# Five rows of wo, each loaded as one stretch of 32 KB or as 16 parts of 1984 bytes and 16 of 64

## The chip, the core and the metric

The kernel runs on one core of a Trainium2 chip. The metric is the device time of one execution, in microseconds (us). Times are medians of several executions; one more execution was recorded by the profiler, and its trace is what the views show. "Span" is the time from the first to the last instruction of that recorded execution, and every start in a view counts from the span's start.

## What is computed

One token (x, 512 wide) goes through two branches, which a gate mixes: attention over a cache of 4096 positions with 32 heads of 128, and a two-layer network with a squared ReLU. All data are bf16.

```
g = sigmoid((x * gate_w).sum(-1))
q = (x @ wq).reshape(32 heads, 128)
scores[h] = k_cache[h] @ q[h] * 128 ** -0.5        # 4096 positions
o[h] = softmax(scores[h]) @ v_cache[h]
a = o.reshape(4096) @ wo                           # wo: 4096 x 512
b = relu(x @ w1 + b1) ** 2 @ w2 + b2               # 512 -> 1376 -> 512
out = g * a + (1 - g) * b
```

Nearly all of the bytes are K and V (32 heads of 1 MB each, twice); wq and wo are 4 MB each, w1 and w2 1.4 MB each.

## The kernel before

The kernel is written engine by engine: each engine has a list of its own, and semaphores tie the lists together.

**Loads.** SyncE (SP) issues wq, then the K and V loads of all heads, K seven heads ahead of V (`load_k` L262, `load_v` L267). Each is one DMA of 1024 KB onto 128 partitions, 8 KB a partition. K and V each have 8 buffers; a K load waits until head h-8 is done with (`s_sd`, `s_t`), a V load until the products of head h-8 are (`s_pv`). Between these loads SP issues w1 (after head 8), the first part of w2 (after head 10), ten pieces of wo (with heads 20 to 24), and behind the last V load the rest of w2 (L294, L295) and the last quarter of wo into the freed K buffer 0 (L297, two DMAs). The output goes out at L301.

**wo.** The first 24 heads' part of wo is 96 rows of 32 KB in the view `woa_v` (one row is 32 rows of wo side by side). Each row goes onto one partition of `W`, the buffer that wq has left. Which row goes to which partition is a table: 13 runs are issued by GpSimd (`RUNS`, L326), 5 groups of three rows by SP (`FIRST`, L279: three partitions of 4 x 8 KB), and 5 single rows by SP (`REST`, L283), onto the partitions 12, 13, 14, 15 and 44. With each of the heads 20 to 24 SP issues V of that head, K seven heads on, one `FIRST` group and one `REST` row, in this order. The ten SP pieces count on one semaphore, `s_wr`.

**A head's work.** VectorE makes half of the scores from K in place (`ttr`, L634), TensorE transposes the other half of K (L435), ScalarE copies it out (L369), and TensorE multiplies it by q (L446). After the maximum and the exponentials (L640, L643, L380) TensorE makes the product with V (`pv`, L471), seven heads behind K. In TensorE's list, step i holds `transposes(i)`, `scores(i-1)` and `pv(i-7)`, so it waits at K of head i and then at V of head i-7.

**The end.** At step 33 the outputs of the first 24 heads are spread over the partitions (L503). From there the attention's first 24 heads go through wo: TensorE takes 23 of the 32 blocks (`out_a`, L515, in steps 34 to 38), VectorE the other 9 (`part_y`, L681 and L684), whose sum TensorE adds in step 37 (`sum_y`, L543). Both wait for all pieces of `W` first (`s_wp`, `s_wr`). `sum_y` stands behind `pv(30)` and ahead of `out_a(5)` and `pv(31)`. Then come the norm of the last 8 heads (L661), their turn (L521, L717, L525, L719), the rest of w2 (L552), the last quarter of wo (`out_b`, L534), the bias (L722), a transpose (L597, L724) and the output.

Of the kernel before, what the change touches and what calls it, by code (L numbers as in the profile page):

```python
# [5 lines left out]
def bass_gated_mix__gqa_block_cached__dense_activation_squared_relu__decode_kernel(  # L6
# [58 lines left out]
    FIRST = [(INNER, 0, 3, 0, 1), (INNER, 0, 3, 1, 1), (INNER, 0, 3, 2, 1), (INNER, 0, 3, 3, 1),  # L65
             (OUTER, 0, 3, 0, 1)]
    REST = [12, 13, 14, 15, 44]
# [11 lines left out]
    def turns():  # L79
        at, out = 0, []  # L80
        for _, e, k, _, _ in RUNS:
            d = (e - at) % 16
            out.append((False, d) if d != 1 else (True, e))
            at = (e + k) % 16
        return out
# [14 lines left out]
    woa_v = A_wo.rearrange("(p t) n -> p (t n)", t=32)  # L100
# [5 lines left out]
    with ctx:  # L106
        def sb(name, shape, dt):
            return ctx.enter_context(nc.sbuf_tensor(name, shape, dt))
# [4 lines left out]
        def sem(name):  # L113
            return ctx.enter_context(nc.semaphore(name))
# [3 lines left out]
        W = sb("W", [128, 4 * 4096], bf16)  # L118
# [72 lines left out]
        s_wr = sem("s_wr")  # L191
# [61 lines left out]
        @block.sync  # L253
        def _(eng):
            for t in range(4):
                eng.dma_start(wq_sb[:, t, :], wq_v[:, t, :]).then_inc(s_wq[t], 16)  # L256

            def load_k(h):
                if h >= NK:
                    eng.wait_ge(s_sd, h - NK + 1)  # L260
                    eng.wait_ge(s_t, 2 * (h - NK + 1))
                eng.dma_start(Kt[:, h % NK, :], k_h[h, :, :]).then_inc(s_k[h % NK], 16)  # L262

            def load_v(h):
                if h >= NV:
                    eng.wait_ge(s_pv, h - NV + 1)
                eng.dma_start(Vt[:, h % NV, :], v_h[h, :, :]).then_inc(s_v[h % NV], 16)  # L267

            for h in range(LAG):
                load_k(h)  # L270
            for h in range(NH):
                load_v(h)
                if h + LAG < NH:
                    load_k(h + LAG)
                if h == HF:
                    eng.wait_ge(s_qps, 8)
                if HF <= h < HF + len(FIRST):
                    p, st, k, q = STRIPS[len(RUNS) + h - HF]
                    eng.dma_start(W[p:p + st * (k - 1) + 1:st, :], woa_v[q:q + k, :],  # L279
                                  max_dma_last_dim=8192).then_inc(s_wr, 16)  # L280
                if HF <= h < HF + len(REST):
                    p, _, _, q = STRIPS[len(RUNS) + len(FIRST) + h - HF]
                    eng.dma_start(W[p:p + 1, :], woa_v[q:q + 1, :],  # L283
                                  max_dma_last_dim=2048).then_inc(s_wr, 16)
                if h == 8:
                    eng.wait_ge(s_z, 1)
                    eng.wait_ge(s_b2, 1)
                    for t in range(4):
                        eng.dma_start(w1_sb[:, t, :], w1_v[:, t, :]).then_inc(s_w1, 16)
                if h == 10:  # L290
                    eng.dma_start(w2a[:, 0:GS[1], :], w2_v[:, 0:GS[1], :]).then_inc(s_w2[0], 16)
            eng.wait_ge(s_sd, NA + 1)
            eng.wait_ge(s_t, 2 * (NA + 1))
            eng.dma_start(w2b[:, :], B_w2[FG * 128:F, :]).then_inc(s_w2[1], 16)  # L294
            eng.dma_start(w2a[:, GS[1]:FG, :], w2_v[:, GS[1]:FG, :]).then_inc(s_w2[2], 16)  # L295
            for c in range(len(TS) - 1):
                eng.dma_start(wob_sb[:, TS[c]:TS[c + 1], :],  # L297
                              wob_v[:, TS[c] * DM:TS[c + 1] * DM].rearrange("p (t n) -> p t n", n=DM))\
                   .then_inc(s_wo[c], 16)
            eng.wait_ge(s_f4, 1)  # L300
            eng.dma_start(out[0, 0, :].rearrange("(j p) -> j p", p=128), fin4[:, :]).then_inc(s_out, 16)  # L301
            eng.wait_ge(s_out, 16)
# [92 lines left out]
        def _(eng):  # L395
# [111 lines left out]
            def out_a(n):  # L507
                if n == 0:
                    eng.wait_ge(s_ac, 2)
                    for q in s_wp:  # L510
                        eng.wait_ge(q, 16)
                    eng.wait_ge(s_wr, 16 * (len(FIRST) + len(REST)))
                for t in range(4 * n, min(4 * n + 4, TD)):
                    for j in range(4):
                        eng.matmul(acc[:, j:j + 1], wo_sb[:, t, j * 128:(j + 1) * 128],  # L515
                                   o2A[:, t:t + 1], start=False, stop=False,
                                   skip_group_check=True)
# [42 lines left out]
            for i in range(NH + LAG):  # L560
# [12 lines left out]
                if i == 34:  # L573
                    out_a(0)
                if 34 <= i < 39:
                    out_a(i - 33)
# [24 lines left out]
        def _(eng):  # L601
# [16 lines left out]
            def qcol_copy(c):  # L618
                eng.wait_ge(s_q, c + 1)
                eng.tensor_copy(qcol[:, 4 * c:4 * c + 4], Q).then_inc(s_qc, 1)  # L620
# [6 lines left out]
            def ttr(h):  # L627
                eng.wait_ge(s_k[h % NK], 16 * (h // NK + 1))
                eng.wait_ge(s_qb, h // 4 + 1)
                if h >= NS:  # L630
                    eng.wait_ge(s_e, h - NS + 1)
                for b in range(XB):
                    kb = Kt[:, h % NK, b * 128:(b + 1) * 128]
                    ins = eng.tensor_tensor_reduce(kb, kb, qb[:, h * 128:(h + 1) * 128], 1.0, 0.0,  # L634
                                                   ALU.mult, ALU.add, S[:, h % NS, b:b + 1])
                ins.then_inc(s_sd, 1)

            def smax(h):
                eng.wait_ge(s_s2, h + 1)
                eng.tensor_copy(S[:, h % NS, XB:NB], S2).then_inc(s_cp, 1)  # L640
                eng.wait_ge(s_cp, h + 1)
                eng.wait_ge(s_sd, h + 1)
                eng.tensor_reduce(mp[:, h:h + 1], S[:, h % NS, :], AX.X, ALU.max).then_inc(s_mp, 1)  # L643

            def gmax(g):
                eng.wait_ge(s_mt, g + 1)
                eng.tensor_reduce(gm[:, g:g + 1], MT[0:G, :], AX.X, ALU.max).then_inc(s_gm, 1)
                eng.wait_ge(s_gm, g + 1)
                eng.tensor_scalar(dg[:, g, :], identf[0:G, 0:G], gm[:, g:g + 1], -SCALE, ALU.mult, ALU.mult)\
                   .then_inc(s_dg, 1)  # L650

            def recip(c):
                a, b = HPO * c, HPO * c + HPO
                eng.wait_ge(s_den, c + 1)
                eng.reciprocal(rden[:, a:b], DEN[:, a:b]).then_inc(s_rd, 1)

            def norm(c):
                a, b = HPO * c, HPO * c + HPO
                eng.wait_ge(s_rd, c + 1)
                eng.wait_ge(s_pv, b)  # L660
                eng.scalar_tensor_tensor(out=onorm[:, a:b], in0=O(a, b), scalar=gcol[:, 0:1],  # L661
                                         in1=rden[:, a:b], op0=ALU.mult, op1=ALU.mult)\
                   .then_inc(s_on, 1)
# [23 lines left out]
            for i in range(NH + LAG):  # L687
                if i < NH:
                    ttr(i)
                if 1 <= i <= NH:  # L690
                    smax(i - 1)
                if i % 3 == 2 and i // 3 + 1 < 8:
                    qcol_copy(i // 3 + 1)
                if i >= 5 and (i - 5) % 4 == 0 and (i - 5) // 4 < NG:
                    gmax((i - 5) // 4)
                if i >= 12 and (i - 12) % HPO == 0:
                    recip((i - 12) // HPO)
                if i >= LAG + 1 and (i - LAG - 1) % HPO == HPO - 1:
                    norm((i - LAG - 1) // HPO)
                if i == 25:  # L700
                    mlp()
                if i == 32:
                    eng.wait_ge(s_at, 1)
                    eng.tensor_copy(oA[:, :], KP[2][0:NA, 0:128]).then_inc(s_ac, 1)
                if i == 33:
                    eng.wait_ge(s_at, 2)
                    eng.tensor_copy(o2A[:, :], O2A).then_inc(s_ac, 1)
                    eng.wait_ge(s_e, NS * 2)
                    eng.tensor_copy(o2D, O2A[:, TD:32]).then_inc(s_y2, 1)
                    for q in s_wp:  # L710
                        eng.wait_ge(q, 16)
                    eng.wait_ge(s_wr, 16 * (len(FIRST) + len(REST)))
                    eng.wait_ge(s_y2, 1)
                    part_y()
            norm(NH // HPO - 1)
# [37 lines left out]
```

## Time and profile before

| what | value |
|---|---|
| median of 3 runs | 207.82 us (207.66 to 207.99) |
| the profiled execution | 207.87 us |
| its span | 206.1 us |
| bytes moved by DMA | 78.76 MB, mean 382 GB/s |
| DMA engines in slices 2 to 36 of 40 | busy 90% or more |
| busy share of PE, DVE, ACT, POOL | 65%, 67%, 39%, 15% |
| TensorE clock granted, mean | 0.58 |

The views used are these. The page gives the span in 40 slices with the mean busy share of the core's 16 DMA engines, the DMA queues with their packets, and the chain of work that ended last. The table of windows gives for each stretch the busy time of each engine, the granted TensorE clock, the share of the 16 DMA engines that was busy, and GB/s. The timeline gives instructions in order of time: start, duration, engine, line, operation, operands, and in brackets how long the engine had been idle and what ended that. "SPq" is SyncE's queue of DMA issues; its durations are the issue alone, not the transfer.

### The profile page before, as it was taken

The numbers are of one execution on the slowest core, as the hardware profiler recorded it, in microseconds if no ns is written. First come the engines' busy times: TensorE is split into PE (matmuls) and PEld (weight loads), VectorE is DVE, ScalarE is ACT, GpSimd is POOL, SyncE is SP. The second block draws the span as 40 slices with busy tenths as digits, with TensorE's granted clock in tenths as the row PEclk, the third lists the DMA queues.
The fourth block names the chain that finished last, engine by engine and source line by source line (L and its number), as shares of the span: only waits on it lengthen the run. The fifth ranks groups of instructions, "written<-read, shape, count | busy, mean of one in ns | idle before, by whom it ended". The sixth has DMA issues, their size and how long they took to land.

```text
span 206.1 us, 6574 instructions
## 1 busy us (share of the span) xinstructions
PE 133.4 (65%) x2405; PEld 118.5 (57%) x2405; DVE 138.7 (67%) x1151; ACT 79.6 (39%) x148; POOL 30.6 (15%) x56
## 2 busy tenths in 40 slices
PE   0139577699967667266596727689987606457585
PEld 0107456287865665156466727579986606447584
DVE  0308999999997687078557737776799926445901
ACT  2106836395553445133363316330763306112000
POOL 2000000000000000000069700001987500000000
PEclk9999957555555855555555555555555555555555
DMA  6999999999999999999999999999999999999100
GB/s 238 425 428 425 418 420 421 415 426 412 421 418 415 423 400 431 409 424 423 413 426 410 420 406 411 417 404 417 407 417 406 407 420 409 420 411 366 64 35 11
DMA packets 12652, 78.76 MB, mean 382 GB/s; under 512 B 2423, under 2 KB 2521, under 8 KB 3546
## 3 DMA queue, kind: packets, MB, share of 16 engines
q1 hardware_dynamic: 11149, 75.83, 89.6%
q0 software_dynamic: 1456, 2.50, 3.3%
q8 instruction: 19, 0.31, 0.6%
q14 instruction: 14, 0.11, 0.1%
q10 hardware_dynamic: 14, 0.01, 0.0%
HBM read 78.32 MB, written 0.00 MB: 380 GB/s over the span
## 4 chain that ended last, share of the span: by engine, by line
DMA 75%; DVE 13%; PE 6%; SPq 4%; issue 1%; ACT 0%; DVEq 0%
DMA Kt<-in_A_k_cache_dram 55%; DMA Vt<-in_A_v_cache_dram 14%; DVE Kt L634 11%; DMA W<-in_A_wq_dram 5%; SPq L267 2%; SPq L262 1%; PE KP L435 1%; PE pQ L413 1%; PE pQ L471 1%; PE pX L543 1%; DVE S L634 1%; SPq L256 1%; PE pX L534 0%; PE pO L471 0%; ACT qb L361 0%
## 5 line engine op out<-in xcount | busy, mean ns | idle before, releaser
L634 DVE CUSTOM_DVE_ANT_0 Kt<-Kt,qb 128x128 bf16<-128x128 bf16 x512 | 113.3, 291 | 33.7 <-DMA Kt<-in_A_k_cache_dram 33.7
L369 ACT ACTIVATE kT<-KP 128x1024 bf16<-128x1024 bf16 x64 | 61.9, 1021 | 77.9 <-PE KP L435 77.9
L435 PE MATMUL KP<-ident,Kt 128*128 128x128 bf16 x512 | 56.1, 297 | 42.9 <-DMA Kt<-in_A_k_cache_dram 42.9
L435 PEld LDWEIGHTS KP<-ident,Kt 128*128 128x128 bf16 x512 | 48.8, 138 | 45.6 <-DMA Kt<-in_A_k_cache_dram 44.5
L634 DVE DVE_READ_ACCUMULATOR2_ANT S<- 128x1 f32 x512 | 42.0, 82 | 0.0
L446 PE MATMUL pS<-qcol,kT 128*128 128x1 bf16 x512 | 19.2, 167 | 8.4 <-DVE S L640 8.4
L446 PEld LDWEIGHTS pS<-qcol,kT 128*128 128x128 bf16 x512 | 18.9, 107 | 9.8 <-DVE S L640 9.8
L323 POOL DMA_DIRECT2D xb<-in_B_w_dram x9 | 5.4, 598 | 102.8 <-PE pQ L413 102.8
L413 PE MATMUL pQ<-W,xb 128*128 128x512 bf16 x32 | 14.9, 621 | 6.3 <-DMA W<-in_A_wq_dram 6.3
L471 PEld LDWEIGHTS pO<-E,Vt 128*128 128x128 bf16 x512 | 15.5, 104 | 1.1 <-issue 0.8
L471 PE MATMUL pO<-E,Vt 128*128 128x1 bf16 x512 | 16.1, 165 | 0.0
L341 POOL TENSOR_SCALAR_AFFINE_SELECT w_sb<-w_sb 24x36 bf16<-24x36 bf16 (+6 forms) x23 | 12.1, 528 | 3.7 <-POOL w_sb L341 0.5
L471 PE MATMUL pQ<-E,Vt 128*128 128x1 bf16 x256 | 8.0, 165 | 5.7 <-DMA Vt<-in_A_v_cache_dram 5.7
L471 PEld LDWEIGHTS pQ<-E,Vt 128*128 128x128 bf16 x256 | 7.6, 104 | 6.3 <-issue 6.0
L361 ACT ACTIVATE qb<-pQ 128x512 bf16<-128x512 f32 x8 | 4.7, 591 | 15.1 <-PE pQ L413 15.1
L380 ACT ACTIVATE E<-S,nM 128x32 bf16<-128x32 f32 x32 | 9.9, 310 | 0.3
L413 PEld LDWEIGHTS pQ<-W,xb 128*128 128x128 bf16 x32 | 3.6, 130 | 10.8 <-issue 10.8
L471 PEld LDWEIGHTS pX<-E,Vt 128*128 128x128 bf16 x256 | 7.9, 105 | 0.7 <-issue 0.6
L471 PE MATMUL pX<-E,Vt 128*128 128x1 bf16 x256 | 8.1, 166 | 0.0
L326 POOL DMA_DIRECT2D W<-in_A_wo_dram x13 | 7.3, 564 | 0.0
L640 DVE COPY S<-pS 128x16 f32<-128x16 f32 x32 | 5.4, 170 | 2.4 <-PE pS L446 2.4
L620 DVE CAST qcol<-pQ 128x4 bf16<-128x4 f32 x8 | 1.2, 153 | 8.4 <-PE pQ L421 8.4
(83 smaller groups left out, 90.1 us busy)
## 6 DMA issues: line engine op xcount, KB each, us to landing
Kt<-in_A_k_cache_dram SPq DMA_DIRECT2D x32, 1024.0 KB, 27.6
Vt<-in_A_v_cache_dram SPq DMA_DIRECT2D x32, 1024.0 KB, 28.8
W<-in_A_wq_dram SPq DMA_DIRECT2D x4, 1024.0 KB, 7.7
W<-in_A_wo_dram POOLq DMA_DIRECT2D x2, 768.0 KB, 12.9
w_sb<-in_B_w_dram SPq DMA_DIRECT2D x4, 344.0 KB, 22.7
w2a<-in_B_w_dram SPq DMA_DIRECT2D x1, 896.0 KB, 21.2
Kt<-in_A_wo_dram SPq DMA_DIRECT2D x1, 768.0 KB, 24.2
W<-in_A_wo_dram POOLq DMA_DIRECT2D x9, 64.0 KB, 23.0
```

Of the source, the lines that this page charges most:

```text
L323: eng.dma_start(dm[0:d, sent, :, 0:8], src[:, :, 0:8]).then_inc(s_dm[sent], 16)
L326: eng.dma_start(W[p:p + st * (k - 1) + 1:st, :], woa_v[q:q + k, :], max_dma_last_dim=8192).then_inc(s_wp[n], 16)
L341: eng.affine_select(out=part, in_=part, compare_op=ALU.not_equal, fill=1.0, base=-st * q, pattern=[[st, 4], [-1, st * (k - 1) + 1]], chann ...
L361: eng.activation(qb[:, c * 512:(c + 1) * 512], pQ[:, :], ACT.Copy).then_inc(s_qb, 1)
L369: eng.activation(kT[:, h % 2, j * HB * 128:(j + 1) * HB * 128], KP[n % 3][:, :], ACT.Copy).then_inc(s_ev, 1)
L380: eng.activation(E[:, h % NE, :], S[:, h % NS, :], ACT.Exp, bias=nM[:, h:h + 1], scale=SCALE, accum_out=RS[:, h:h + 1]).then_inc(s_e, 1)
L413: mm = eng.matmul(pQ[:, :], xb[:, t, :], wq_sb[:, t, c * 512:(c + 1) * 512], start=(t == 0), stop=(t == 3))
L435: mm = eng.transpose(KP[n % 3][:, y * 128:(y + 1) * 128], Kt[:, h % NK, b * 128:(b + 1) * 128], ident[:, :])
L446: mm = eng.matmul(S2[:, y:y + 1], kT[:, h % 2, y * 128:(y + 1) * 128], qcol[:, h:h + 1], start=True, stop=True)
L471: mm = eng.matmul(O(h, h + 1), Vt[:, h % NV, b * 128:(b + 1) * 128], E[:, h % NE, b:b + 1], start=(b == 0), stop=(b == NB - 1))
L634: ins = eng.tensor_tensor_reduce(kb, kb, qb[:, h * 128:(h + 1) * 128], 1.0, 0.0, ALU.mult, ALU.add, S[:, h % NS, b:b + 1])
L640: eng.tensor_copy(S[:, h % NS, XB:NB], S2).then_inc(s_cp, 1)
```

## The change

Each of the five single rows (`REST`) is seen as 16 pieces of 1024 elements, on both sides. One DMA takes the first 992 elements of every piece (1984 bytes), a second the last 32 (64 bytes). So each row is 32 stretches instead of one, and SP issues two DMAs instead of one. The same bytes go to the same partitions, and the place in SP's list is the same. The two waits for `s_wr` (in `out_a` on TensorE, and ahead of `part_y` on VectorE) count the five more DMAs.

```
-                    eng.dma_start(W[p:p + 1, :], woa_v[q:q + 1, :],
-                                  max_dma_last_dim=2048).then_inc(s_wr, 16)
+                    to, of = [m.rearrange("p (s n) -> p s n", s=16) for m in (W[p:p + 1, :], woa_v[q:q + 1, :])]
+                    for x, y in ((0, 992), (992, 1024)):
+                        eng.dma_start(to[:, :, x:y], of[:, :, x:y]).then_inc(s_wr, 16)
...
-                    eng.wait_ge(s_wr, 16 * (len(FIRST) + len(REST)))
+                    eng.wait_ge(s_wr, 16 * (len(FIRST) + 2 * len(REST)))
```

SP's list around the first of the five rows, before and now (`Kt` and `Vt` are the buffers of K and V, `W` that of wo; the line numbers behind the change are one higher):

```order
 L262 DMA Kt<-in_A_k_cache_dram 128x4096
 L279 DMA W<-in_A_wo_dram 3x4x4096
-L283 DMA W<-in_A_wo_dram 1x16384
+L285 DMA W<-in_A_wo_dram 1x16x992
+L285 DMA W<-in_A_wo_dram 1x16x32
 L267 DMA Vt<-in_A_v_cache_dram 128x4096
 L262 DMA Kt<-in_A_k_cache_dram 128x4096
 L279 DMA W<-in_A_wo_dram 3x4x4096
-L283 DMA W<-in_A_wo_dram 1x16384
+L285 DMA W<-in_A_wo_dram 1x16x992
+L285 DMA W<-in_A_wo_dram 1x16x32
```

One issue has become two, at the same place; no other instruction of any engine has moved.

More of the change, by code (lines that the diff above doesn't have):

```diff
@@ L711, in _ @@
                         eng.wait_ge(q, 16)
-                    eng.wait_ge(s_wr, 16 * (len(FIRST) + len(REST)))
+                    eng.wait_ge(s_wr, 16 * (len(FIRST) + 2 * len(REST)))
                     eng.wait_ge(s_y2, 1)
```

## The prediction

> **What bounds the kernel now.** I read the page first (the slices, the queues, the chain), then windows over the end, then the timelines of TensorE, VectorE and SyncE's issues. The page's slices, queues and chain:
>
> ```profile
> span 206.1 us, 6574 instructions
> ...
> DMA  6999999999999999999999999999999999999100
> ...
> q1 hardware_dynamic: 11149, 75.83, 89.6%
> q0 software_dynamic: 1456, 2.50, 3.3%
> ...
> DMA 75%; DVE 13%; PE 6%; SPq 4%; issue 1%; ACT 0%; DVEq 0%
> ```
>
> The DMA engines are busy from the second slice to the end of the 36th, and three quarters of the chain that ended last are loads. TensorE and VectorE follow the loads. What matters is thus when the last loads land, and the end shows that they do not land on all 16 engines alike. Windows over the end (after the counts of the five engines come the TensorE clock, the busy share of the 16 DMA engines, and GB/s):
>
> ```profile
> 178.00:190.00 12.00, 8.23 (x200) 7.61 (x201) 6.43 (x44) 3.44 (x11) 0.00 (x0) 0.50 1.00 395
> 191.50:197.30 5.80, 3.67 (x110) 3.56 (x111) 4.08 (x7) 0.00 (x0) 0.00 (x0) 0.50 0.14 52
> 197.30:202.60 5.30, 4.80 (x108) 4.50 (x106) 0.58 (x3) 0.00 (x0) 0.00 (x0) 0.50 0.07 27
> 202.60:206.10 3.50, 1.36 (x42) 1.09 (x39) 0.40 (x3) 0.00 (x0) 0.00 (x0) 0.50 0.00 0
> ```
>
> One engine of 16 is a share of 0.06, two are 0.13. Until 190 all work. From 191.5 to 197.3 it is two, from 197.3 to 202.6 a single one, then none. So one engine, here called the last one, ends 5.3 us behind the second and over 11 us behind the other fourteen, and a load has landed only when its slowest engine is through. TensorE's list shows the same from its side (the number behind x is of instructions; in brackets the idle time and what ended it):
>
> ```profile
> 161.39 1.89 PE L435 MATMUL KP<-ident,Kt 128*128 128x128 bf16 x16 [2.15 <-DMA Kt<-in_A_k_cache_dram]
> 169.83 1.89 PE L435 MATMUL KP<-ident,Kt 128*128 128x128 bf16 x16 [5.08 <-DMA Kt<-in_A_k_cache_dram]
> 178.23 1.89 PE L435 MATMUL KP<-ident,Kt 128*128 128x128 bf16 x16 [4.65 <-DMA Kt<-in_A_k_cache_dram]
> ...
> 184.34 1.00 PE L471 MATMUL pQ<-E,Vt 128*128 128x1 bf16 x32 [1.91 <-DMA Vt<-in_A_v_cache_dram]
> ...
> 197.00 0.99 PE L471 MATMUL pQ<-E,Vt 128*128 128x1 bf16 x32 [0.56 <-DMA Vt<-in_A_v_cache_dram]
> 197.85 1.85 PE L543 MATMUL pX<-onesf,kT 128*128 128x1 f32 x8
> 199.56 0.46 PE L515 MATMUL pX<-o2A,W 128*128 128x1 bf16 x12
> 199.88 0.99 PE L471 MATMUL pQ<-E,Vt 128*128 128x1 bf16 x32
> ...
> 202.69 1.00 PE L534 MATMUL pX<-o2B,Kt 128*128 128x1 bf16 x32
> ```
>
> The V loads of heads 25 to 30 come in one behind the other, (197.00 - 184.34) / 5 = 2.53 us apart: the time of one load on the last engine, which carries a sixteenth of it, 64 KB. The K loads of heads 29, 30 and 31 are 8.44 and 8.40 us apart, though only K, V, a `FIRST` group and a `REST` row lie between them.
>
> **Who carries the stretch.** The packet count of queue 1 tells. SP issues 76 loads on 128 partitions (4 of wq, 32 of K, 32 of V, 4 of w1, and 2 each of w2 and wo's last quarter): 9728 packets. w2's rest is 96, the `FIRST` groups 5 x 12, the output 4. If each engine that takes part in a DMA adds one small packet that raises the semaphore, there are 77 x 16 + 5 x 3 + 4 = 1251 of these. That makes 11139, and 11149 are counted: ten are left for five rows, so a row is one packet and one small one, on one engine. The 32 KB are not shared out at all. [...]
>
> **Part one: the last engine loses the stretches.** Between two K loads it carries K and V (2 x 2.53 = 5.06 us), its row of a `FIRST` group (32 KB, half a load's share, 1.27), and the stretch: 8.40 - 5.06 - 1.27 = 2.07 us. Five are 10.4 us. The lower bound is the plain rate, 32 KB in 1.27 us, or 6.4 in all. By either value this engine falls behind the second: 202.6 - 10.4 = 192.2, or 202.6 - 6.4 = 196.2, against 197.3. So the gain is not 10.4; it ends at the second engine, 5.3 us at most.
>
> **Part two: every engine gets a sixteenth.** A row now brings each engine 1984 bytes, 64 bytes and two small packets. 2 KB of a load's 64 KB are 2.53 / 32 = 0.08 us. For the small ones the page's queue 0 is the nearest row: 3.3% of 16 x 206.1 is 108.8 us; 2.50 MB are 305 packets of 8 KB at 2.53 / 8 = 0.316, or 96.4 us; the other 1151 share 12.4 us, 11 ns each. So 0.08 + 3 x 0.011 = 0.11 us a row, 0.56 us for five, on every engine. On the fourteen that end by 191.5 it is hidden by their lead. On the second it is on the path: 197.3 becomes 197.9. The lower bound is nothing; a gain is excluded here, since no engine but the last loses bytes. The upper bound is that the parts of a row stand in each other's way, all going to one partition: then each engine is held for 1.27 to 2.07 us a row. I take 0.11, since the engines do not come to the row together: at the end they stand 5 and 6 us apart, against 1.27. [...]
>
> **Part three: SP's issues.**
>
> ```profile
> 126.04 0.90 SPq L279 DMA_DIRECT2D W<-in_A_wo_dram  x1
> 126.99 0.37 SPq L283 DMA_DIRECT2D W<-in_A_wo_dram  x1
> ...
> 153.82 20.12 SPq L267 DMA_DIRECT2D Vt<-in_A_v_cache_dram  x7
> ...
> DMA to landing us min/median/max: 20.9/28.8/34.7
> ```
>
> A row's issue takes 0.37 us where nothing blocks it, a three-dimensional one like L279's 0.90. Two of the latter instead of one of the former cost up to 1.4 us, 7 us for five rows. Queued behind them in SP's list are the next V and K loads. What hides this: V loads (the last row is theirs) land 21 us or more after their issue, so the engines have that much queued. [...] I cost it at nothing; without the cover it would be 7 us. The two waits on `s_wr` count to a higher number and cost nothing; the rows land earlier than before.
>
> **The sum.** The second engine carries the same loads in the same order behind the rows, so V of heads 30 and 31 and the last weights land as much earlier as it is ahead of the last one: 5.3 - 0.6 = 4.7 us. From V of head 30 to the end TensorE's list has no gap that another load fills: `pv(30)` at 197.00, `sum_y`, the last `out_a`, `pv(31)` at 199.88, `out_b` from 202.69. All of it moves by 4.7, if what stands ahead follows. TensorE's waits for V say whether it can:
>
> ```profile
> L471 PE MATMUL pQ<-E,Vt 128*128 128x1 bf16 x229 | 7.3, 165 | 5.7 <-DMA Vt<-in_A_v_cache_dram 5.7
> ...
> 188.76 0.49 DVE L681 TENSOR_SCALAR kT<-W,S 128x512 f32<-128x512 bf16 x1 [0.43 <-DVE S L709]
> 189.28 6.26 DVE L684 SCALAR_TENSOR_TENSOR kT<-W,S,kT 128x512 f32<-128x512 bf16 x8
> ```
>
> Between K of head 31 and `pv(30)` TensorE idles 5.7 us for V alone. Even if that K came no earlier, it could come up by 5.7, more than the 4.7. `part_y` on VectorE ends at 195.54, and `sum_y`, which needs it, starts at 197.85; this is 2.3 us of slack, and it starts behind the V wait of head 26, which moves too. So the span goes from 206.1 to 201.4. The profiled execution took 207.87, 1.77 more than its span and 0.05 more than the median of the runs; 207.87 - 4.7 = 203.2, beside the median 203.1.
>
> **The rivals.**
>
> *The rows jam (slower).* All 16 parts of a row go to one partition. If every engine is held until the row is in, the second pays 5 x 1.27 = 6.4 us and ends at 203.7, 1.1 us behind where the last one ends now: 209.0; at 2.07 a row, 207.7 and 213.0. It decides from 5.3 / 5 = 1.06 us a row on the second engine. For it speaks the 2.07; against it that the second engine comes several us behind the fourteen. [...] Chance 0.06. *Half a jam*, 0.6 us a row, leaves 197.3 + 3.0 = 200.3, a gain of 2.3: 205.6. Chance 0.09.
>
> *The row stays on one engine (slower or the same).* If all parts still go to the last engine, it saves nothing and gets 31 more packets a row, at up to 11 ns: 5 x 0.34 = 1.7, so 207.9 to 209.6. For it: 16 pieces lie in one partition, and no load of this trace is cut like that. Chance 0.06.
>
> *VectorE or TensorE becomes the bound.* If K of head 31 moves by 2 us only and the chain behind it could not use the V waits, the end would move by 2: 205.9. Against it stand the 5.7 us. Chance 0.04.
>
> **How the numbers follow.** The forecast, 203.1, has 0.75; its own range is 202.2 to 204.2 (rows that cost nothing, 207.8 - 5.3 = 202.5, and a little for V of head 30 coming still earlier; at the other end 0.3 us a row). About 0.2% is what a measurement of this kernel can tell from no change. Faster by more: 0.75 + 0.09 + 0.04, less a little for a jam near the break-even, 0.87; within it 0.03 (a jam at 1 us a row, or a row on one engine with cheap packets); slower 0.10. To 205.6 the range takes in the weaker jam and leaves out less than 0.2.
>
> **What would show it.** Queue 1's packets: 11139 + 5 x 64 = 11459 if each part gets an engine of its own with its small packets, 11309 if all stay on one (32 packets and two small ones a row). Windows: no stretch with a single busy engine 5 us long, the last load done near 197.9. K of heads 30 and 31 no longer 8.4 us apart. `pv(30)` near 192.3, `part_y` done before 193.1. The prediction is wrong if the fourteen engines end far behind 191.5 (a jam), or if TensorE waits for something else than V between 184 and 197.

## The result and the profile after

The change makes the kernel faster: 202.28 us median (202.06 to 202.53, 6 runs) against 207.89 us (207.66 to 208.03, 6 runs), a ratio of 0.9732 with a 95% interval of 0.9719 to 0.9744. The prediction was 203.1 us in a range of 202.2 to 205.6, so the result lies close to the low end of the range. The profiled execution took 202.31 us, its span is 200.5 us, 5.6 less than before.

From the page after, the slices and queue 1:

```profile
span 200.5 us, 6579 instructions
...
DMA  6999999999999999999999999999999999999940
...
q1 hardware_dynamic: 11459, 75.83, 92.5%
```

The bytes of queue 1 are the same, and its packets are the 11459 that were worked out for 16 engines with two parts and two small packets each, five times. The slices end in "9940" instead of "9100": most of the DMA engines now stop close to the end. The windows over the end (columns as before):

```profile
178.00:190.00 12.00, 8.36 (x255) 7.80 (x252) 8.81 (x25) 1.67 (x10) 0.00 (x0) 0.50 1.01 400
190.00:191.50 1.50, 1.14 (x30) 1.09 (x28) 0.21 (x1) 0.00 (x0) 0.00 (x0) 0.50 0.97 386
191.50:193.70 2.20, 2.20 (x39) 2.20 (x39) 0.00 (x0) 0.00 (x0) 0.00 (x0) 0.50 0.51 195
193.70:197.00 3.30, 2.80 (x76) 2.50 (x76) 0.55 (x3) 0.00 (x0) 0.00 (x0) 0.50 0.08 30
197.00:200.50 3.50, 1.40 (x43) 1.12 (x40) 0.44 (x3) 0.00 (x0) 0.00 (x0) 0.50 0.00 0
```

Before, two engines were left at 191.5 and one from 197.3 to 202.6. Now one engine is left from 193.7 to 197.0, and all others end between 191.5 and 193.7. No view names an engine. The experiments below bear out this reading: the engine that ended at 202.6 is among those that are done by 193.7, and what was the second is now the last; it ends at 197.0 where it ended at 197.3 before. TensorE's list (K waits, then the end):

```profile
162.43 1.89 PE L436 MATMUL KP<-ident,Kt 128*128 128x128 bf16 x16 [2.73 <-DMA Kt<-in_A_k_cache_dram]
169.00 1.89 PE L436 MATMUL KP<-ident,Kt 128*128 128x128 bf16 x16 [3.21 <-DMA Kt<-in_A_k_cache_dram]
175.10 1.89 PE L436 MATMUL KP<-ident,Kt 128*128 128x128 bf16 x16 [2.36 <-DMA Kt<-in_A_k_cache_dram]
...
191.44 0.99 PE L472 MATMUL pQ<-E,Vt 128*128 128x1 bf16 x32 [0.36 <-DMA Vt<-in_A_v_cache_dram]
192.29 1.84 PE L544 MATMUL pX<-onesf,kT 128*128 128x1 f32 x8
...
194.32 0.99 PE L472 MATMUL pQ<-E,Vt 128*128 128x1 bf16 x32
197.12 1.00 PE L535 MATMUL pX<-o2B,Kt 128*128 128x1 bf16 x32
```

`pv(30)` starts at 191.44 instead of 197.00, 5.56 us earlier, and from there to the span's end it takes 9.06 us, as it did before (9.10). So the whole difference of the spans has arisen by the time V of head 30 lands. The K loads of the last heads are 6.57 and 6.10 us apart, no longer 8.4. That is still more than two loads of 2.53 us each, and this is the thread that the experiments pull.

### The profile page after: what moved, and what is told of

Its sections match the earlier page's. It is cut to its first block, busy times and chain, and to the rows that moved or that the text cites. A ratio compares the mean times of both kernels' runs of the same rounds, so it can differ in the third digit from the quotient of the medians.

```text
span 200.5 us, 6579 instructions
## 1 busy us (share of the span) xinstructions
PE 134.5 (67%) x2405; PEld 119.6 (60%) x2405; DVE 138.9 (69%) x1151; ACT 79.5 (40%) x148; POOL 30.6 (15%) x56
## 3 DMA queue, kind: packets, MB, share of 16 engines
q1 hardware_dynamic: 11459, 75.83, 92.5%
## 4 chain that ended last, share of the span: by engine, by line
DMA 59%; DVE 16%; SPq 12%; PE 9%; issue 2%; ACT 0%; DVEq 0%
DMA Kt<-in_A_k_cache_dram 41%; DVE Kt L635 14%; DMA Vt<-in_A_v_cache_dram 13%; DMA W<-in_A_wq_dram 5%; SPq L262 4%; SPq L267 3%; SPq L285 3%; PE KP L436 2%; PE pQ L414 2%; PE pQ L472 1%; DVE S L635 1%; SPq L279 1%; PE pO L472 1%; PE pX L544 1%; PE pS L447 1%
## 5 line engine op out<-in xcount | busy, mean ns | idle before, releaser
L436 PE MATMUL KP<-ident,Kt 128*128 128x128 bf16 x512 | 57.1, 300 | 38.5 <-DMA Kt<-in_A_k_cache_dram 38.5
L436 PEld LDWEIGHTS KP<-ident,Kt 128*128 128x128 bf16 x512 | 49.6, 140 | 41.2 <-DMA Kt<-in_A_k_cache_dram 40.1
L635 DVE DVE_READ_ACCUMULATOR2_ANT S<- 128x1 f32 x512 | 41.3, 81 | 0.0
```

Of the source, the lines that this page charges most:

```text
L436: mm = eng.transpose(KP[n % 3][:, y * 128:(y + 1) * 128], Kt[:, h % NK, b * 128:(b + 1) * 128], ident[:, :])
```

## The experiments

Each run is set against the kernel before on the same chip; medians of the first four belong to 208.03 us, of the last two to 208.08 us. The theory: one engine carried all five stretches at 2.07 us each, and the gain ends where the next engine ends. The edits are shown against the changed kernel, or against the kernel before where the text says so; the counts in the two waits for `s_wr`, which follow the number of DMAs, are left out.

Some readings below use one source more. The trace keeps each DMA packet with its start, duration and size, but not its engine. The views do not print these packet records, so their numbers stand in the text.

| run | median, us | ratio to before (95%) |
|---|---|---|
| two_rows_cut | 203.91 | 0.9804 (0.9788 to 0.9821) |
| one_engine_parts | 209.93 | 1.0090 (1.0071 to 1.0108) |
| no_rows | 197.61 | 0.9500 (0.9485 to 0.9514) |
| other_partitions | 199.62 | 0.9592 (0.9572 to 0.9612) |
| whole_rows_elsewhere | 207.94 | 0.9994 (0.9983 to 1.0004) |
| five_engines | 199.04 | 0.9568 (0.9554 to 0.9583) |

**Two of the five rows cut** (two_rows_cut): is the gain one of steps up to a stop, or a fifth for each row?

```
     HF = 20
+    CUT = 2
...
+                    if h >= HF + CUT:
+                        eng.dma_start(W[p:p + 1, :], woa_v[q:q + 1, :],
+                                      max_dma_last_dim=2048).then_inc(s_wr, 16)
...
-                    for x, y in ((0, 992), (992, 1024)):
+                    for x, y in ((0, 992), (992, 1024)) if h < HF + CUT else ():
```

> Only the first two of the five rows are cut into 16 parts of 1984 bytes and 16 of 64; the other three stay one stretch. Theory 1 (each stretch costs the last engine 2.07 us, and the gain ends only where the second engine ends): the last engine saves 2 x 2.07 = 4.1 us less 0.2 us of parts, still behind the second, so about 207.9 - 3.9 = 204.0 us. Rival (the gain is spread evenly over the rows, each a fifth of 5.6 us): 207.9 - 2.2 = 205.7 us.

203.91 us, as the theory has it; the rival's 205.7 is out. Its windows show the two engines at the end 1 us apart (0.13 is two engines, 0.06 one):

```profile
192.60:197.50 4.90, 4.24 (x89) 4.07 (x89) 0.28 (x2) 0.00 (x0) 0.00 (x0) 0.50 0.13 53
197.50:198.50 1.00, 0.89 (x30) 0.79 (x28) 0.32 (x2) 0.00 (x0) 0.00 (x0) 0.50 0.06 23
```

The last engine ends at 198.5 instead of 202.6, 4.1 us earlier for two rows, 2.05 each; the second stays at 197.5. Two rows bring 4.1 us, the other three only 1.6 more: the stop is the second engine.

**All parts on one engine** (one_engine_parts): each row as 17 parts of 1856 bytes, 17 of 64 and a rest of 128 bytes. That these would stay on one engine was the author's estimate; queue 1's packets, below, show that they did.

```
-                    to, of = [m.rearrange("p (s n) -> p s n", s=16) for m in (W[p:p + 1, :], woa_v[q:q + 1, :])]
-                    for x, y in ((0, 992), (992, 1024)):
+                    to, of = [m[:, 0:16320].rearrange("p (s n) -> p s n", s=17) for m in (W[p:p + 1, :], woa_v[q:q + 1, :])]
+                    for x, y in ((0, 928), (928, 960)):
                         eng.dma_start(to[:, :, x:y], of[:, :, x:y]).then_inc(s_wr, 16)
+                    eng.dma_start(W[p:p + 1, 16320:], woa_v[q:q + 1, 16320:]).then_inc(s_wr, 16)
```

> [...] Theory 1 (what counts is that one engine carries the row): no gain, 207.9 us, up to 209.6 us with 11 ns for each small packet. Rival (a single packet of 32 KB is slow by itself, 2.07 us instead of 1.27 at the rate of a load, and short parts are not): the last engine saves 5 x 0.8 = 4 us, so 204 us.

209.93 us, 1.9 us slower than before and 0.3 us above the upper end of what was expected. The count says that the parts did stay together (11329 is the 11139 packets of the kernel without rows, and 5 x 38 for 35 parts and three small packets a row), and the windows that one engine again ends far behind:

```profile
q1 hardware_dynamic: 11329, 75.83, 89.2%
```

```profile
197.50:204.90 7.40, 6.39 (x148) 6.03 (x146) 0.94 (x5) 0.00 (x0) 0.00 (x0) 0.50 0.08 30
204.90:208.30 3.40, 1.32 (x41) 1.05 (x37) 0.37 (x2) 0.00 (x0) 0.00 (x0) 0.50 0.00 0
```

So cutting by itself saves nothing. The stretch was not slow because it was long: as parts it is no faster. The packet records agree: before, the 32 KB packet of a row took 1.94 us (1.88 to 1.99), and here the 17 parts of 1856 bytes took 1.90 us together (1.77 to 2.01). They also show where the time goes. The first parts of a row take 76 ns each, about the rate of a load (72 ns for 1856 bytes at 2.53 us for 64 KB), and most of the later ones 150 to 165 ns, twice as long. A row's 34 more parts and 2 more small packets cost 1.9 / 5 = 0.38 us, 10.6 ns each if all cost the same (an estimate had been 11). The rival is out. By the packets of queue 1 a row of 16 parts took 16 engines (11459), one of 17 parts one engine (11329), and a single stretch of 16384 elements one engine (11149). What decides the number was not shown.

**No rows at all** (no_rows): the five rows are not loaded, the issue is taken out and the two waits count 5 x 16. What do the parts cost?

```
-                    to, of = [m.rearrange("p (s n) -> p s n", s=16) for m in (W[p:p + 1, :], woa_v[q:q + 1, :])]
-                    for x, y in ((0, 992), (992, 1024)):
-                        eng.dma_start(to[:, :, x:y], of[:, :, x:y]).then_inc(s_wr, 16)
+                    pass
```

> The five rows are not loaded at all, so five of the 96 rows of the first 24 heads' part of wo are missing from the output. Theory 1 with parts that cost the second engine 0.11 us a row: 202.3 - 0.6 = 201.7 us, with a second engine that still ends about 6 us behind the fourteen. Rival A (parts are free): 202.3 us. Rival B (the second engine is the one that writes the partitions 12 to 15 and 44 to 47, and it is the rows, whoever carries them, that hold it back, about 1.1 us each): it comes up by 5.5 us and the end is then set by the fourteen and by TensorE, about 197 to 198 us.

197.61 us, 4.7 less than with the parts, as rival B had it, and not my 0.6. Without the rows all engines are through by 192.4, most of them by 191.5:

```profile
190.00:191.50 1.50, 0.90 (x22) 0.74 (x20) 0.44 (x2) 0.00 (x0) 0.00 (x0) 0.50 0.58 228
191.50:192.40 0.90, 0.73 (x25) 0.66 (x22) 0.17 (x1) 0.00 (x0) 0.00 (x0) 0.50 0.18 61
192.40:195.60 3.20, 1.13 (x33) 0.86 (x31) 0.38 (x2) 0.00 (x0) 0.00 (x0) 0.50 0.00 0
```

And TensorE's K waits of heads 29 to 31 are 4.98 and 4.93 us apart, no more than the two loads of 2.53 us each. The `FIRST` groups still lie between them and do not show:

```profile
160.34 1.89 PE L434 MATMUL KP<-ident,Kt 128*128 128x128 bf16 x16 [1.36 <-DMA Kt<-in_A_k_cache_dram]
165.32 1.89 PE L434 MATMUL KP<-ident,Kt 128*128 128x128 bf16 x16 [1.62 <-DMA Kt<-in_A_k_cache_dram]
170.25 1.89 PE L434 MATMUL KP<-ident,Kt 128*128 128x128 bf16 x16 [1.19 <-DMA Kt<-in_A_k_cache_dram]
```

So there is nothing behind the second engine's 5.8 us of lag but the rows. Measured from 192.4, by which every engine is done without them, they cost it at least (197.3 - 192.4) / 5 = 0.98 us a row before, when it carried none of their bytes, and (197.0 - 192.4) / 5 = 0.92 us a row after, when it carries a sixteenth.

The packet records of the kernel before show how it loses this time. Beside each 32 KB packet there is one other engine whose 8 KB packets take about 0.62 us instead of the usual 0.31, three or four in a row. It loses 1.1 to 1.2 us by this, 5.9 us over the five rows, which is the second engine's whole lag of 5.8. The row's own later parts took twice as long too (150 to 165 ns instead of 76), as seen above. That two writers share one place, each at half its rate, is the author's estimate from these two doublings; no view names the place.

**The rows on other partitions** (other_partitions, whole_rows_elsewhere): the same edit, once in the changed kernel and once in the kernel before.

```
-    REST = [12, 13, 14, 15, 44]
+    REST = [7, 11, 17, 101, 113]
```

> The five rows are cut as in the changed kernel, but go to the free partitions 7, 11, 17, 101 and 113 instead of 12, 13, 14, 15 and 44; the table of the other rows is unchanged. Theory 1 without a shared place of writing: nothing changes, 202.3 us. Rival B (rows on the partitions 12 to 15 and 44 to 47 hold back the engine that writes these for the loads, and this is the second engine): the second engine comes up by up to 5.5 us, so 197 to 198.5 us, with no engine ending 4 us behind the rest.

> The kernel before (each row one stretch of 32 KB), but with the rows on the free partitions 7, 11, 17, 101 and 113 instead of 12, 13, 14, 15 and 44. Theory (the last engine is the one that carries the stretches, 2.07 us each, and the second engine is held back by writes of others to its own partitions, wherever these come from): the last engine shares with another engine now and keeps its 2.07 us, so the time stays at 207.9 us within 0.5, while the second engine comes up by 5 us, so that a single busy engine is left from about 192 on. Rival (the stretch is slow because of the engine of the partitions 12 to 15 alone): the stretch falls to 1.27 us, the last engine saves 4 us, 204 us.

Cut, the rows cost 2.0 us on these partitions (199.62 against 197.61) and 4.7 on the old ones. The last engines end at 194.8, where in the changed kernel one engine alone was busy from 193.7 to 197.0:

```profile
192.00:194.00 2.00, 1.50 (x44) 1.22 (x42) 0.44 (x2) 0.00 (x0) 0.00 (x0) 0.50 0.42 166
194.00:194.80 0.80, 0.80 (x28) 0.73 (x26) 0.17 (x1) 0.00 (x0) 0.00 (x0) 0.50 0.13 41
194.80:198.10 3.30, 1.22 (x33) 0.95 (x33) 0.37 (x2) 0.00 (x0) 0.00 (x0) 0.50 0.00 0
```

That is 1.1 us more than the 198.5 at the upper end of what rival B had. Whole, they leave the time where it was (207.94), and one engine alone is busy from 192.6 on:

```profile
191.50:192.60 1.10, 0.38 (x14) 0.41 (x15) 1.03 (x3) 0.00 (x0) 0.00 (x0) 0.50 0.27 106
192.60:202.80 10.20, 8.08 (x204) 7.67 (x201) 3.63 (x8) 0.00 (x0) 0.00 (x0) 0.50 0.08 30
```

The pair separates the two engines. The last one pays 2 us a row wherever the rows go, so it is the carrier, and the rival with 204 us is out. The second is late only when the rows go to partitions 12 to 15 and 44: from 197.3 it comes up to 192.6 at the latest and this changes no time there, since the last engine hides it. That the second engine is the one which writes these partitions for the loads is what the runs speak for; no view names an engine, and none of the five rows went onto 45 to 47 in any run. With the rows whole and elsewhere the packet records still show packets of about 0.62 us beside every row, so each row still holds up an engine. That none of these ends late speaks for another engine each time.

**A row for each of five engines** (five_engines): from the kernel before, the five rows become one more group of the other table, and the list of single rows is empty.

```
-             (OUTER, 0, 3, 0, 1)]
-    REST = [12, 13, 14, 15, 44]
+             (OUTER, 0, 3, 0, 1), (OUTER, 1, 5, 3, 1)]
+    REST = []
...
```

> The five rows as one DMA onto the partitions 7, 11, 15, 19 and 23, four parts of 8 KB each, issued with head 25: five partitions, so five engines, a row each, each writing partitions that another engine writes too. Theory (a row costs the engine that carries it 1.3 to 2.1 us and the one that writes its partitions about 1.1 us; what counts is the engine that ends last): the five engines lose 2 to 3 us once instead of five times 2.07 us on one, and the fourteen are not held up five times; the engine of the partitions 12 to 15 loses about 1.1 us instead of 5.5. About 198.5 us. Rival (what saves time is the cut into small parts): the time goes back towards that before, 203 us or more.

199.04 us, the fastest kernel of this study that loads all rows, and without any small part. Queue 1 counts the 11139 packets of the kernel without rows and 25 more, which are 20 parts of 8 KB and a small packet for each of five engines. All engines are through at 193.9:

```profile
q1 hardware_dynamic: 11164, 75.83, 93.8%
```

```profile
190.00:192.00 2.00, 1.83 (x48) 1.74 (x47) 0.07 (x1) 0.00 (x0) 0.00 (x0) 0.50 0.85 319
192.00:193.90 1.90, 1.56 (x37) 1.29 (x38) 0.54 (x3) 0.00 (x0) 0.00 (x0) 0.50 0.27 100
193.90:197.20 3.30, 1.19 (x33) 0.92 (x32) 0.37 (x2) 0.00 (x0) 0.00 (x0) 0.50 0.00 0
```

The rival is out. This run changes the engines, the partitions and the number of issues at once, so it does not say which of them brings the 3.2 us over the changed kernel.

## Why the prediction was right, and where it was not

**What bounds it.** Right. One engine of 16 ended 5.3 us late, and the load waits of TensorE follow the slowest engine (the last engine's end came up from 202.6 to 197.0, and `pv(30)` from 197.00 to 191.44). All of the gain is in place when V of head 30 lands.

**Who carries the stretch.** Right: 11459 packets with 16 parts, 11329 with 17 on one engine, which then ended at 204.9. That each of the 16 engines gets a sixteenth of a cut row, a term of the sum, no run had shown when the sum was made; the 11459 packets show it.

**Part one, 2.07 us a row on the last engine.** Right in size: two rows took 4.1 us off it. Right too that the gain ends at the second engine: the other three rows brought 1.6 us.

**Part two, 0.11 us a row on every engine, with the second on the path.** This is the term that was mis-sized. I had the second engine move from 197.3 to 197.9; it moved to 197.0, and the 0.9 us between is the gap between the forecast gain, 4.7, and the measured 5.6. The step that failed is the sentence that no engine but the last could gain, since no other lost bytes. The second engine pays for the rows by being held up: 0.98 us a row before, and 0.92 after with its own share of the bytes in it, so it is held up a little less and this pays for the bytes. The prediction took the second engine's 5.8 us behind the fourteen as given and did not ask where they came from. My 0.11 is not the price of a row; without the rows at all the kernel is 4.7 us faster, where I had 0.6. That the forecast came within 0.9 us is in part luck: the price that it did not know, about 1 us a row on the second engine, was there before and after and nearly cancels.

**The upper bound of part two, the jam.** It exists, on engines where it is hidden. The fourteen ended by 191.5 before and by 193.7 now, 2.2 us later for five rows, 0.44 us a row and not 0.11. They had 5.5 us to spare up to the second engine. I had kept the jam out of the sum because the engines would not come to a row together. In the packet records they do: of the 16 long parts 8, 8 and 11 start within 0.4 us of each other, at about 160, 165 and 170 us. The parts take 81 to 125 ns each, but right behind the last group, from 170.7 to 171.2 us, 16 packets of 8 KB are under way that take 0.5 to 1.05 us instead of 0.31, as many as there are engines. The second engine's end moves with the partitions the rows go to and not with who carries them: 197.3 with whole rows on 12 to 15 and 44, 197.0 with cut ones there, and 192.6 at the latest with whole rows elsewhere. That these partitions share one place of writing was not shown.

**Part three, SP's issues at nothing.** Right as far as the traces show. The five pairs of issues took 13.8 us of SP's time where the five single ones had taken 8.7, but the DMA engines never ran dry: they are busy 90% or more in every slice from the second to the 38th. The last pair takes 2.27 us, and the V loads behind the last row are issued at the same time as before (153.46 against 153.82):

```profile
151.15 2.27 SPq L285 DMA_DIRECT2D W<-in_A_wo_dram  x2
153.46 19.63 SPq L267 DMA_DIRECT2D Vt<-in_A_v_cache_dram  x7
...
DMA to landing us min/median/max: 20.9/27.4/31.8
```

**What stands ahead follows.** Right, with the cover that was named: TensorE's idle time for V behind K of head 31 fell from 5.7 to 2.4 us, and `part_y` begins its long part at 182.97 instead of 189.28, done before `sum_y` at 192.29.

```profile
L472 PE MATMUL pQ<-E,Vt 128*128 128x1 bf16 x250 | 8.0, 165 | 3.0 <-DMA Vt<-in_A_v_cache_dram 2.4 <-issue 0.5
...
182.97 6.26 DVE L685 SCALAR_TENSOR_TENSOR kT<-W,S,kT 128x512 f32<-128x512 bf16 x8
```

What stays open is part of the price that is left: the rows still cost 2.0 us when cut onto other partitions, and 1.4 us on five engines. The bytes and small packets of the cut rows are 0.55 us an engine (an estimate, 5 x 0.11). The packet records give most of the rest: the 8 KB packets that start behind 140 us took, by engine, 1.27 us more in all than in the run without rows (1.36 us more in the changed kernel). So the rows also slow down other packets where they go to five places. Why cut rows slow down engines that write other partitions was not tried by itself.

## What to carry to other kernels

Where loads set the end, ask how many DMA engines are busy in the last microseconds: a share of 0.06 is a single one, and then the work is to be shared out, not shortened. Count packets to see whether a DMA is spread: here one onto a single partition, contiguous on both sides, stayed on one engine (11149 packets), 16 parts took all engines (11459), 17 took one (11329), and five partitions took five (11164). And look at where bytes are written as well as at who carries them: five rows onto partitions 12 to 15 and 44 held up an engine that carried none of them by at least 0.98 us each, and another choice of partitions, or one row on each of five engines, was worth 2.7 to 3.2 us more than the changed kernel's cut.

## What the hardware showed that was not expected

An engine that carried none of a row's bytes lost about 1 us to a row of 32 KB (at least 0.98 us by the ends, 1.1 to 1.2 us by its packets, which took 0.62 us instead of 0.31). Five rows onto partitions 12 to 15 and 44 held up one engine five times, to 197.3; with the whole rows elsewhere no engine but the carrier ended later than 192.6. The carrier paid about 2 us a row (2.05 by the ends in two_rows_cut, 1.94 by its packets) instead of the 1.27 of its plain rate (half of a load's 2.53), and with whole rows elsewhere it ended at 202.8, as late as the 202.6 before. And parts of 64 bytes took 11 ns and the small packets of a DMA 9 ns in the packet records (10.6 ns each by the slower run with 17 parts), so cutting small was cheap here.
